# Sliding-window attention into a leaky-ReLU layer: the row sums of the softmax taken from pre-added overlaps, early values loaded four heads at a time, and two banks for the first units of chunk 9

## Chip, cores and metric

The kernel runs on one core of a Trainium2 chip. The metric is the device time of one execution in microseconds. Several runs are made and their median is the time of the kernel; one further execution is recorded by the hardware profiler, and the views below come from that one.

## What is computed

The reference is banded attention followed by a two-layer block. `q`, `k` and `v` are 8 batches x 8 heads x 576 positions x 64.

```
scores = q k^T / 8, kept where 0 <= i - j < 32            (heads 0 to 3, "plain")
                    or 0 <= i - j < 128 and i - j = 0 mod 4 (heads 4 to 7, "dilated")
attn   = softmax over the kept keys
x      = attn v, heads side by side: 4608 x 512
out    = max(0.01 h, h) w_out,  h = x w_in      (512 -> 2048 -> 512)
```

Inputs and output are float32; the products run on float16 operands.

## The kernel before

**Attention in units.** Two heads that are worked together make a "visit" (`VISITS`, two dilated ones first, then two plain ones), and a visit has two units of 288 queries (`unit`, L685). The keys of a unit stand in blocks of 64 per head (128 rows for the two heads), and a block meets only the queries that can see it: `steps` (L702 to L720) lists five blocks, each with its stretch of queries, 96, 80, 64 or 32 columns wide. Since a query in the overlap of two blocks is needed by both, the five stretches have 384 columns for 288 queries in a dilated unit and 416 in a plain one. A unit then runs: scores on TensorE (L732), exp on ScalarE into `ee` (L739), the mask as a product with a table in `con` on VectorE (L743; batches 0 and 1 add the mask on TensorE instead, L728), the product with a matrix of ones that gives the row sums (`t_sum_`, L754) and the product with the values (`t_v`, L756). Both of these are made by `second` (L747): five matmuls, one a block, that add into one bank at the place of their queries. Then come log and exp of the sums on ScalarE (L761, L763) and a multiplication into `xt` on VectorE (L774). There are 64 units, 8 in each batch.

**The two layers.** The tokens go in 12 chunks of 384. `up` (L784) makes the first layer of a chunk in 16 blocks of four matmuls. Chunks 9 to 11 use a Winograd-Strassen form with seven products (`up_seven`, L1157), each unit of it on three banks that go round in `last_seven` (L1244). `down` (L820) makes the second layer of the first four tiles plainly; all others go in groups of four through another seven-product form (`group`, L872; L922).

**Loads.** Batches 0 and 1 (`EARLY`) are loaded in an order written out by hand, `FIRST` (L29): `w0` to `w7` are pieces of `w_in`, `w8` to `w15` of `w_out`, `q` and `v` with batch and half are queries with keys and values (half 1 is the dilated heads), `r` is the last 64 positions, `c` is the mask table, and each "." is a further DMA of a `v` load named before. For a dilated half `load_v` (L510 to L516) makes six DMAs, and four casts of 64 x 576 (L521) put the values in their places. All of these are issued on SyncE's queue, in order; a DMA whose buffer is still in use holds back all behind it.

**What orders the work.** Nothing is executed as the Python calls come. Every operation is a task with engines that may take it, a cost, a delay and its dependencies (`add`, L76), and `_Plan.run` (L228) lists them: a forward pass places each task at the time when its engine is free, with the lowest due time first, a backward pass makes new due times, and the best of nine passes gives each engine one fixed order. `MARGIN`, `CALM`, `WHEN` and `RAMP` scale these costs and due times. A task that two engines may take goes to the one that ends it first by the plan. On the chip an engine runs its list in order and waits at each entry for its inputs.

Of the kernel before, what the change touches and what calls it, by code (L numbers as in the profile page):

```python
# [26 lines left out]
def _margin(name, at):  # L27
    return MARGIN[name] if at > CALM else 1.0
FIRST = ('w0 q01 r0 v01 . q00 . . . . w1 v00 . w2 w3 w4 w5 w6 w7 q11 r1 q10 v11 w8 w9 . '  # L29
         'w10 v10 . . . w11 . w12 . w13 . c . w14 w15')  # L30


def _constants():

    ident = np.eye(128, dtype=np.float16)
    key = np.arange(128)[:, None] % 64
    rel = np.arange(96)[None, :] - key
    band = (rel >= 0) & (rel < WIN)
# [6 lines left out]
    plain1 = [band] * 3 + [band[:, :64], band[:, 32:]]  # L45
# [204 lines left out]
def kernel(  # L250
# [54 lines left out]
    vst = [sbuf(f"vst{i}", [128, 1152], FP32) for i in range(NVS)]  # L305
    slots = sbuf("slots", [128, NT * TS])
    turned = [sbuf(f"turned{i}", [128, 640]) for i in range(NX)]
    ee = [sbuf(f"ee{i}", [128, 512]) for i in range(NE)]
# [180 lines left out]
    def load_v(b, g, prio, at_step=None):  # L489
# [5 lines left out]
        def when(x):  # L495
            n[0] += 1
            return at_step[n[0] - 1] if at_step else prio + x
        for hh in range(2):
# [184 lines left out]
    bank_at = [0]  # L683

    def unit(b, vi, u, prio, banks):  # L685
# [14 lines left out]
        if dil:  # L700
            n, steps = 384, []
            for ab in range(2):  # L702
                for r in range(2):
                    w = (96, 80)[ab]
                    steps.append((4 * ab + 2 * u + r, [[1, w]], (2 * u + r) * 144 + 64 * ab,
                                  96 * r if ab == 0 else 192 + 80 * r, w,
                                  144 * r + 64 * ab, [[1, w]]))
            steps.append((8, [[144, 2], [1, 16]], 2 * u * 144 + 128, 352, 32, 128, [[144, 2], [1, 16]]))
            bias = [(0, 192, 0, [[0, 2], [1, 96]]), (192, 160, 0, [[0, 2], [1, 80]]),
                    (352, 32, 96 + 32 * u, [[1, 32]])]  # L710
        elif u == 0:
# [3 lines left out]
            bias = [(0, 384, 0, [[0, 4], [1, 96]]), (384, 32, 0, [[1, 32]])]  # L715
        else:
            n = 416
            steps = [(s, [[1, 96]], 64 * s, 96 * (s - 5), 96, 64 * s - 288, [[1, 96]]) for s in (5, 6, 7)]
            steps.append((8, [[1, 64]], 512, 288, 64, 224, [[1, 64]]))
            steps.append((4, [[1, 64]], 288, 352, 64, 0, [[1, 64]]))  # L720
            bias = [(0, 288, 0, [[0, 3], [1, 96]]), (288, 64, 0, [[1, 64]]), (352, 64, 32, [[1, 64]])]
# [32 lines left out]
        t_sum_ = add("PE", 0.188, 0.25, [t_m, t_e, t_id], second(p_bank, lambda s: block_ones),  # L754
                     prio, 0.4, "z")
# [116 lines left out]
    def group(four, acts, at_time, split):  # L872
# [33 lines left out]
        def add_up(dst, a, b, op, deps, who, t_late=0.0):  # L906
            t = add("DVE", 0.63 if n_g > 3 else 0.78, 0.2, deps,
                    lambda e: ENG[e].tensor_tensor(out=dst, in0=a, in1=b, op=op),  # L908
                    at_time - 8 + t_late, 0.0, "A")
            for i in who:  # L910
                used[i].append(t)
            return t
# [134 lines left out]
    for i, step in enumerate(steps):  # L1047
        if step[0] == "v":
            rows[step] = [clock[0] + 1 + i]
            waiting += [step] * {"v01": 5, "v11": 5, "v00": 1, "v10": 3}[step]  # L1050
# [44 lines left out]
    U_SEVEN = (9, 10, 11)  # L1095
    HF, HT = DFF // 2, 192
# [60 lines left out]
    def up_seven(c, j0, batches, ts, acc, banks, when):  # L1157
# [70 lines left out]
        p7 = product(w_sum_of(3), x_sum_of(3), "Z", True, [s_t[3], ts[3][2]], 3)  # L1228
# [15 lines left out]
    def last_seven():  # L1244
# [8 lines left out]
        for order, c in enumerate(U_SEVEN):  # L1253
            batches = [[c // 3 * 2], [c // 3 * 2, c // 3 * 2 + 1], [c // 3 * 2 + 1]][c % 3]
            ts = x_sums(c, batches, order)
            for n in range(4):
                banks = [ready.pop(0) for _ in range(3)]
                up_seven(c, 2 * n, batches, ts, all_acts[c], banks, begins[c] + 2.5 * n)
                ready += before + [banks[1]]
                before = [banks[0], banks[2]]  # L1260

    n_g = 0
    for m in range(B // 2):
# [4 lines left out]
        if 3 * m not in U_SEVEN:  # L1268
            ups(3 * m, 0, 384, [e])
        if m == 0:  # L1270
# [6 lines left out]
        else:  # L1277
            attend(o, WHEN[o], 6.5)
            if 3 * m + 1 not in U_SEVEN:
                ups(3 * m + 1, 0, 384, [e, o])  # L1280
        if 3 * m + 2 not in U_SEVEN:
# [10 lines left out]
        while n_g < len(groups) and all(all_acts[c][0] for c, _ in groups[n_g]):  # L1292
            four = groups[n_g]
            group(four, all_acts, begins[four[-1][0] + 1] + four[-1][1] * 2.0, n_g == len(groups) - 1)
            n_g += 1
# [56 lines left out]
```

## Time and profile before

| What | us |
| --- | --- |
| median of 3 runs | 304.04 (304.03 to 304.31) |
| the profiled execution | 303.41 |
| span of its records | 301.5 |
| TensorE busy in the span | 288.6 |
| VectorE, ScalarE busy | 218.7, 217.1 |
| GpSimd busy | 136.7 |

The span is from the first to the last record; 1.9 us of the profiled execution lie outside it. PE is TensorE's matmuls, PEld its weight loads, DVE VectorE, ACT ScalarE, POOL GpSimd and SP SyncE; a "q" after a name means the engine's queue of instructions. L754 and the like are lines of the kernel. In a timeline a row has start, length, engine, line, operation, tiles, shape, count, and in brackets the idle time before it with what ended it. The length of a matmul includes its way through the array, so what a row of matmuls costs is better read from the chain of work or from the start of the next row.

### The profile page before, as it was taken

How to read it: one execution, taken by the hardware profiler on the slowest of the kernel's cores; microseconds unless marked ns; L12 is line 12 of the kernel's file. 1: busy time of each engine (PE TensorE's matmuls, PEld its weight loads, DVE VectorE, ACT ScalarE, POOL GpSimd, SP SyncE). 2: the span in 40 equal slices, each digit the busy share in tenths (PEclk: the TensorE clock that was granted, in tenths of full speed). 3: DMA queues.
4: the chain of work that ended last, by engine and by line, in shares of the span. 5: the costliest groups of instructions: out<-in, count | busy, mean ns of one | idle time of the engine just before them, and what ended most of it. 6: DMA issues, size and time to landing. Idle time of an engine off the chain costs nothing.

```text
span 301.5 us, 7912 instructions
## 1 busy us (share of the span) xinstructions
PE 288.6 (96%) x3038; PEld 227.9 (76%) x3038; DVE 218.7 (73%) x386; ACT 217.1 (72%) x509; POOL 136.7 (45%) x194
## 2 busy tenths in 40 slices
PE   5889989899999999999999999999999999999995
PEld 2466666568766789777777777877788999999984
DVE  5586464898568979876747779799964878587832
ACT  1497886568897775799688877688777778868321
POOL 5365434386678948778567984487000000000000
PEclk9999999999999999999999999999999999999999
DMA  7999999979988978997998999771201110011123
GB/s 241 303 339 371 293 275 282 158 152 177 161 176 164 235 160 164 207 163 157 193 167 200 161 219 170 142 183 36 72 2 49 57 37 1 10 65 70 37 104 105
DMA packets 156102, 47.17 MB, mean 156 GB/s; under 512 B 136864, under 2 KB 153376, under 8 KB 156064
## 3 DMA queue, kind: packets, MB, share of 16 engines
q1 hardware_dynamic: 155376, 46.04, 65.8%
q10 hardware_dynamic: 688, 0.63, 0.6%
q8 instruction: 23, 0.38, 0.5%
q14 instruction: 15, 0.12, 0.1%
HBM read 37.22 MB, written 9.44 MB: 155 GB/s over the span
## 4 chain that ended last, share of the span: by engine, by line
PE 81%; DMA 12%; DVE 2%; ACT 2%; SPq 1%; POOL 1%; issue 1%; DVEq 0%; POOLq 0%; ACTq 0%
PE hps L793 26%; PE fps L922 23%; PE tp L922 8%; DMA xt<-in_moe_w_out_dram 5%; DMA stg<-in_q_dram 5%; PE ops L750 4%; PE hps L1185 4%; PE ops L1185 4%; PE fps L832 3%; PE sps L750 2%; DMA vst<-in_v_dram 2%; PE ops L732 2%; PE sps L1185 1%; PE ops L922 1%; PE sps L732 1%; ACT slots L384 1%
## 5 line engine op out<-in xcount | busy, mean ns | idle before, releaser
L793 PE MATMUL hps<-xt,w_in 128*128 128x384 f16 (+1 forms) x616 | 107.4, 309 | 1.2 <-ACT gt L808 0.8
L808 ACT ACTIVATE gt<-hps 128x384 f16<-128x384 f32 (+1 forms) x154 | 69.1, 458 | 21.6 <-PE hps L793 19.8
L922 PEld LDWEIGHTS <-gt 128*128 128x128 f16 x768 | 72.4, 98 | 9.8 <-DVE gt L908 0.3
L793 PEld LDWEIGHTS <-w_in 128*128 128x128 f16 x640 | 56.4, 98 | 26.2 <-issue 1.9
L373 POOL CAST nat<-stg 128x576 f16<-128x576 f32 (+1 forms) x55 | 41.7, 779 | 30.2 <-DMA stg<-in_k_dram 20.7
L373 POOL CAST slots<-vst 64x576 f16<-64x576 f32 x53 | 47.0, 900 | 10.3 <-PE hps L793 4.4
L922 PE MATMUL fps<-w_out,gt 128*128 128x256 f16 x368 | 47.0, 272 | 0.0
L743 DVE TENSOR_TENSOR ee<-ee,con 128x384 f16<-128x384 f16 (+1 forms) x48 | 27.9, 582 | 13.4 <-ACT ee L739 13.1
L763 ACT ACTIVATE rc<-rc 128x288 f32<-128x288 f32 x64 | 27.7, 445 | 1.0
L774 DVE TENSOR_TENSOR xt<-ops,rc 128x288 f16<-128x288 f32 x42 | 18.8, 449 | 11.5 <-ACT rc L763 10.8
L386 POOL COPY slots<-turned 64x64 f16<-64x64 f16 (+2 forms) x41 | 21.6, 531 | 6.3 <-DVE turned L585 1.9
L739 ACT ACTIVATE ee<-ops 128x384 f16<-128x384 f32 (+1 forms) x41 | 20.5, 502 | 5.5 <-PE ops L732 5.5
L750 PEld LDWEIGHTS <-con 128*128 128x128 f16 x320 | 19.1, 98 | 4.8 <-issue 1.0
L732 PEld LDWEIGHTS <-slots 128*128 128x128 f16 x320 | 19.1, 97 | 4.5 <-ACT slots L384 0.2
L951 ACT COPY stg<-fps 128x512 f32<-128x512 f32 (+1 forms) x24 | 12.8, 533 | 11.4 <-PE fps L922 10.2
L750 PEld LDWEIGHTS <-slots 128*128 128x128 f16 x320 | 17.5, 97 | 3.5 <-issue 1.2
L761 ACT ACTIVATE rc<-ops 128x288 f32<-128x288 f32 x41 | 16.7, 411 | 4.1 <-PE ops L750 4.1
L585 DVE STREAM_TRANSPOSE turned<-nat 128x576 f16<-128x576 f16 x24 | 17.9, 760 | 1.3 <-POOL nat L373 1.3
L1212 ACT ACTIVATE gt<-slots 128x384 f16<-128x384 f32 x36 | 17.7, 526 | 1.4 <-DVE slots L1205 1.4
L832 PE MATMUL fps<-w_out,gt 128*128 128x512 f16 x64 | 16.6, 378 | 1.1 <-POOL w_out L373 0.7
L384 ACT COPY slots<-turned 64x576 f16<-64x576 f16 (+1 forms) x24 | 16.0, 666 | 1.1 <-DVE turned L585 0.8
L1185 PEld LDWEIGHTS <-stg 128*128 128x128 f16 x192 | 16.4, 98 | 0.4
(121 smaller groups left out, 504.1 us busy)
## 6 DMA issues: line engine op xcount, KB each, us to landing
out_dram<-osb SPq DMA_DIRECT2D x32, 256.0 KB, 2.6
stg<-in_q_dram SPq DMA_DIRECT2D x48, 144.0 KB, 3.6
stg<-in_k_dram SPq DMA_DIRECT2D x48, 144.0 KB, 3.4
vst<-in_v_dram SPq DMA_DIRECT2D x32, 128.0 KB, 3.1
vst<-in_v_dram SPq DMA_DIRECT2D x14, 288.0 KB, 4.3
gt<-in_moe_w_in_dram SPq DMA_DIRECT2D x6, 512.0 KB, 6.5
stg<-in_q_dram SPq DMA_DIRECT2D x3, 512.0 KB, 7.0
stg<-in_k_dram SPq DMA_DIRECT2D x3, 512.0 KB, 6.5
```

Source lines behind the costliest of these rows:

```text
L373: ENG[e].tensor_copy(out=dst, in_=src)
L386: ENG[e].tensor_copy(out=dst, in_=src)
L732: nc.tensor.matmul(p_bank[:, c:c + w], slot(tn, KB + 128 * s, 0, 128, [1, 128]), slot(tn, qx, 0, 128, *qd), start=first or not by_pe, stop ...
L739: lambda e: nc.scalar.activation(out=et[:, 0:n], in_=p_bank[:, 0:n], func=AF.Exp, scale=SCALE), prio)
L743: lambda e: nc.vector.tensor_tensor(out=et[:, 0:n], in0=et[:, 0:n], in1=con[:, table:table + n], op=ALU.mult), prio,
L750: nc.tensor.matmul(at(dst, 0, 128, o, *od), lhs(s), et[:, c:c + w], start=i == 0, stop=i == len(steps) - 1, skip_group_check=True)
L763: lambda e: nc.scalar.activation(out=rt, in_=rt, func=AF.Exp, scale=-1.0), prio)
L793: nc.tensor.matmul(ht[:, 0:n], at(w_in, 0, 128, vi * DFF + j // 2 * 256 + j % 2, [2, 128]), at(xt[m % 2], 0, 128, vi * 1152 + x0 + x, [1, n]),
L808: lambda e: nc.scalar.activation(out=gt[c % NG][:, j * n_c + x:j * n_c + x + n], in_=ht[:, 0:n], func=AF.Prelu, alpha=0.01),
L832: nc.tensor.matmul(ft, g[:, j * n_c + tt * 128:j * n_c + tt * 128 + 128], w_out[:, j * DM:j * DM + DM], start=(j == 0), stop=(j == NJ - 1))
L922: nc.tensor.matmul(bk[:, x:x + HN], tl[:, off + j * step:off + j * step + 128], rhs(j), start=first and x == 0 and j == 0, stop=j == HJ - ...
L1185: nc.tensor.matmul(b[:, i * HT:i * HT + HT], lhs(v, j0 + i), rhs(v), start=first and i == 0 and v == 0, stop=i == 1 and v == 1, skip_group ...
```

## The change

The query stretches of a unit are added up ahead of the product with ones: one or two additions (`both`) put the sum of two overlapping stretches behind the others in `ee`, at column 448 (`PLUS`), on VectorE or GpSimd. Then each query is streamed once (`sums_of`): 288 columns, in four matmuls (dilated), three (first plain unit) or two (second plain unit). This holds from batch 2 on (`PLUS_FROM`). So that the second plain unit's overlaps lie at one step, its fifth block comes first, in the mask table too.

The values of a dilated half of batches 0 and 1 are loaded in two DMAs in place of six, four heads at once, over 128 rows for the main part; ten casts then move them, eight of 64 x 256 and two of 64 x 128, in place of four. `FIRST` is another order: the first queries ahead of `w0`, the `v` pieces closer to their first one, `c` at the end.

The first two units of chunk 9 use two banks, the second one for both `Y` and `Z`, so that `p7` also waits for the addition that empties `Y`. `down_groups` is called after each `ups` and inside `last_seven`, not once in each turn of the loop. The scales of the plan have other values, and `RAMP` gives the early loads a delay that grows with their place.

```diff
-RAMP = 0
-WHEN = (0.0, 0.0, 40.0, 70.0, 100.0, 125.0, 150.0, 180.0)
+RAMP = 0.83
+WHEN = (0.0, 0.0, 40.0, 70.0, 100.0, 127.2, 150.0, 180.0)
-MARGIN = {'ACT': 1.045, 'DVE': 1.154, 'POOL': 1.018, 'PE': 1.0, 'SP': 1.0, 'DMA': 1.133, 'LAND': 1.15}
-CALM = 49.7
+MARGIN = {'ACT': 1.045, 'DVE': 1.13, 'POOL': 1.041, 'PE': 1.0, 'SP': 1.0, 'DMA': 1.139, 'LAND': 1.15}
+CALM = 38.0
-FIRST = ('w0 q01 r0 v01 . q00 . . . . w1 v00 . w2 w3 w4 w5 w6 w7 q11 r1 q10 v11 w8 w9 . '
-         'w10 v10 . . . w11 . w12 . w13 . c . w14 w15')
+FIRST = ('q01 w0 r0 v01 . q00 w1 v00 . w2 w3 w4 w5 w6 w7 q11 r1 v11 q10 w8 w9 . w10 v10 '
+         'w11 w12 . w13 . . w14 w15 c')
...
+        if g == 1 and b < EARLY:
+            t_main = load("SP", at(vs, 0, 128, 0, [256, 4], [1, 256]),
+                          dram(v, base, [4 * D, 128], [HS, 4], [1, 256]), 512, 1024, v_old, when(0.0))
+            t_last = load("SP", at(vs, 0, 64, 1024, [D, 4], [1, D]),
+                          dram(v, base + 512 * D, [D, 64], [HS, 4], [1, D]), 256, 256, v_old, when(0.01))
...
+            last = [cast(slot(t0, VB + hh + 1024, 64 * hh, 64 * hh + 64, [TS, 2], [2, D]),
+                         at(vs, 0, 64, 1024 + 128 * hh, [D, 2], [1, D]), 128,
+                         [t_last] + old[0] + old[1], prio, ("POOL", "DVE", "ACT"), 1.3) for hh in range(2)]
...
+                made = [cast(slot(t0 + j, VB + hh + 512 * i, 64 * hh, 64 * hh + 64, [128, 4], [2, D]),
+                             at(vs, 64 * i, 64 * i + 64, (2 * hh + j) * 256, [D, 4], [1, D]), 256,
+                             [t_main] + old[j], prio, ("POOL", "DVE", "ACT"), 1.3)
+                        for i in range(2) for hh in range(2)]
...
+            both = [(64, [[96, 2], [1, 32]], 192, [[80, 2], [1, 32]], 0, 32),
+                    (256, [[80, 2], [1, 16]], 352, [[16, 2], [1, 16]], 64, 16)]
+            sums_of = [(0, [[96, 2], [1, 64]], 0, [[144, 2], [1, 64]]),
+                       (PLUS, [[32, 2], [1, 32]], 64, [[144, 2], [1, 32]]),
+                       (224, [[80, 2], [1, 32]], 96, [[144, 2], [1, 32]]),
+                       (PLUS + 64, [[16, 2], [1, 16]], 128, [[144, 2], [1, 16]])]
...
-        t_sum_ = add("PE", 0.188, 0.25, [t_m, t_e, t_id], second(p_bank, lambda s: block_ones),
-                     prio, 0.4, "z")
+        if b < PLUS_FROM:
+            t_sum_ = add("PE", 0.188, 0.25, [t_m, t_e, t_id], second(p_bank, lambda s: block_ones),
+                         prio, 0.4, "z")
+        else:
+            t_both = []
+            for x, dx, y, dy, z, w in both:
...
+                    ENG[e].tensor_tensor(out=at(et, 0, 128, PLUS + z, *dz), in0=at(et, 0, 128, x, *dx),
+                                         in1=at(et, 0, 128, y, *dy), op=ALU.add)
+                t_both.append(add((("DVE", 0.08 + n_w * 0.001), ("POOL", 0.1 + n_w * 0.0011)), None, 0.2,
+                                  [t_m, t_e], fn, prio, 0.0, "m"))
...
+            t_sum_ = add("PE", 0.13, 0.25, [t_m, t_e, t_id] + t_both, add_over, prio, 0.4, "z")
...
-        p7 = product(w_sum_of(3), x_sum_of(3), "Z", True, [s_t[3], ts[3][2]], 3)
+        p7 = product(w_sum_of(3), x_sum_of(3), "Z", True,
+                     [s_t[3], ts[3][2]] + [h11[1]] * (banks[1] is banks[2]), 3)
...
-                banks = [ready.pop(0) for _ in range(3)]
+                if c == 9 and n < TWO:
+                    banks = [hps[n % 2], hps[1 - n % 2], hps[1 - n % 2]]
+                else:
+                    banks = [ready.pop(0) for _ in range(3)]
```

More of the change, by code (lines that the diff above doesn't have):

```diff
@@ L304 @@
     nat = [sbuf(f"nat{i}", [128, 1152]) for i in range(NNAT)]
-    vst = [sbuf(f"vst{i}", [128, 1152], FP32) for i in range(NVS)]
+    vst = [sbuf(f"vst{i}", [128, 1280], FP32) for i in range(NVS)]
     slots = sbuf("slots", [128, NT * TS])
     turned = [sbuf(f"turned{i}", [128, 640]) for i in range(NX)]
-    ee = [sbuf(f"ee{i}", [128, 512]) for i in range(NE)]
+    ee = [sbuf(f"ee{i}", [128, 640]) for i in range(NE)]
     rc = [sbuf(f"rc{i}", [128, 320], FP32) for i in range(NR)]
@@ L683 @@
     bank_at = [0]
+    PLUS, PLUS_FROM = 448, 2
     def unit(b, vi, u, prio, banks):
@@ L906, in add_up @@
         def add_up(dst, a, b, op, deps, who, t_late=0.0):
-            t = add("DVE", 0.63 if n_g > 3 else 0.78, 0.2, deps,
+            t = add("DVE", 0.63 if n_g[0] > 3 else 0.78, 0.2, deps,
                     lambda e: ENG[e].tensor_tensor(out=dst, in0=a, in1=b, op=op),
@@ L1095 @@
     U_SEVEN = (9, 10, 11)
+    TWO = 2
     HF, HT = DFF // 2, 192
@@ L1256, in last_seven, with down_groups @@
             for n in range(4):
-                banks = [ready.pop(0) for _ in range(3)]
-                up_seven(c, 2 * n, batches, ts, all_acts[c], banks, begins[c] + 2.5 * n)
-                ready += before + [banks[1]]
-                before = [banks[0], banks[2]]
-    n_g = 0
+                if c == 9 and n < TWO:
+                    banks = [hps[n % 2], hps[1 - n % 2], hps[1 - n % 2]]
+                else:
+                    banks = [ready.pop(0) for _ in range(3)]
+                    ready += before + [banks[1]]
+                    before = [banks[0], banks[2]]
+                up_seven(c, 2 * n, batches, ts, all_acts[c], banks, begins[c] + 2.5 * n)
+            down_groups()
+    n_g = [0]
+    def down_groups():
+        while n_g[0] < len(groups) and all(all_acts[c][0] for c, _ in groups[n_g[0]]):
+            four = groups[n_g[0]]
+            group(four, all_acts, begins[four[-1][0] + 1] + four[-1][1] * 2.0, n_g[0] == len(groups) - 1)
+            n_g[0] += 1
     for m in range(B // 2):
@@ L1269 @@
             ups(3 * m, 0, 384, [e])
+            if m:
+                down_groups()
         if m == 0:
@@ L1280 @@
                 ups(3 * m + 1, 0, 384, [e, o])
+                down_groups()
         if 3 * m + 2 not in U_SEVEN:
@@ L1291 @@
             part_free[0] = part_free[1] = rings["STG"][-1]
[L1292 to L1295, printed above, removed]
+        down_groups()
     order = plan.run()
```

33 lines of the change are left out of this document (27 added, 6 removed).

## The prediction, made before the result was known

> **What bounds the kernel now.** I read the page first, then busy time by stretches, then the waits of TensorE alone, then the chain of work.
>
> ```profile
> PE 288.6 (96%) x3038; PEld 227.9 (76%) x3038; DVE 218.7 (73%) x386; ACT 217.1 (72%) x509; POOL 136.7 (45%) x194
> ```
> ```profile
> 10.00:20.00 10.00, 7.71 (x107) 5.58 (x108) 6.40 (x15) 6.92 (x18) 5.81 (x8) 1.00 1.13 323
> 20.00:40.00 20.00, 19.25 (x217) 13.87 (x216) 11.99 (x29) 16.59 (x44) 8.96 (x15) 1.00 1.01 332
> 40.00:60.00 20.00, 17.27 (x189) 11.48 (x186) 13.11 (x23) 13.25 (x36) 7.73 (x10) 1.00 1.03 235
> 60.00:200.00 140.00, 139.94 (x1466) 107.43 (x1465) 109.75 (x177) 110.41 (x256) 100.16 (x138) 1.00 0.90 178
> 200.00:296.00 96.00, 96.00 (x1035) 85.52 (x1033) 70.31 (x131) 67.27 (x155) 8.90 (x11) 1.00 0.14 48
> ```
>
> The columns after the stretch are its length, then busy time of PE, PEld, DVE, ACT and POOL with counts, the granted clock, the DMA share and GB/s. From 60 to 296 us TensorE is never idle (139.94 of 140, 96.00 of 96) at full clock: what its list loses there the kernel gains, and a wait put into it is paid in full. Before 60 us it idles: 2.29 us from 10 to 20, 0.75 from 20 to 40, 2.73 from 40 to 60, with the DMA share over 1. So there are two stages, a head set by loads and a body set by TensorE.
>
> ```profile
> PE hps L793 <- ACT gt L808: 0.8, 2, 0.6
> PE fps L832 <- POOL w_out L373: 0.7, 1, 0.7
> ```
> ```profile
> 46.77 8.89 DMA xt<-in_moe_w_out_dram
> 55.66 0.05 issue
> 55.72 0.88 POOL w_out L373
> 56.60 0.04 issue
> 56.64 0.59 PE fps L832 x2
> ```
>
> The last wait that the head hands to TensorE is for `w_out`: its last piece lands at 55.66, POOL casts it, L832 starts at 56.64, and the body begins.
>
> **Part 1: the product with ones.** Here is the chain inside the body, and the count of units that mask on VectorE, which are the units from batch 2 on.
>
> ```profile
> 120.07 0.19 PE sps L750 x5
> 120.25 0.20 PE ops L750 x5
> 120.45 0.88 PE fps L922 x8
> 121.33 0.18 PE ops L750 x5
> 121.52 0.87 PE tp L922 x8
> 122.39 0.18 PE sps L750 x5
> 122.58 0.87 PE fps L922 x8
> 123.45 0.17 PE ops L732 x5
> 123.62 1.31 PE hps L793 x8
> ```
> ```profile
> L743 DVE TENSOR_TENSOR ee<-ee,con 128x384 f16<-128x384 f16 (+1 forms) x48 | 27.9, 582 | 13.4 <-ACT ee L739 13.1
> ```
>
> Eight matmuls of 384 columns take 1.31 us, so a column takes 0.426 ns. A dilated unit drops from 384 to 288 columns (0.041 us), a plain one from 416 to 288 (0.055 us). With 24 units of each, of the 48 that mask on VectorE, that is 0.98 + 1.31 = 2.29 us. A product of five takes 0.19 us on the mean of the four L750 rows, against 0.164 to 0.177 for its columns, so a matmul also has a few ns of its own, and 84 of 240 fall away (four, three or two in place of five). But the new ones are narrower, and no row shows a stretch of 32 or 64 alone. If a narrow one takes as long as one of 96 columns (0.041 us), a dilated product saves 0.01, a first plain 0.05, a second plain 0.065, together 1.6 us. If the time is all columns (0.123 a product), it is 48 x 0.065 = 3.1 us. I take **-2.4**, nearest the column count. It is on the path, since all 48 lie after 60 us.
>
> **Part 2: the head.** The mask table `c` moves behind the last two pieces of `w_out`, and the early dilated values are two DMAs, not six.
>
> ```profile
> 33.41 3.34 SPq L358 DMA_DIRECT2D vst<-in_v_dram  x4
> 44.54 0.63 SPq L358 DMA_DIRECT2D con<-consts  x1
> 45.92 0.74 SPq L358 DMA_DIRECT2D wst<-in_moe_w_out_dram  x1
> 46.77 0.36 SPq L358 DMA_DIRECT2D xt<-in_moe_w_out_dram  x1
> ```
> ```profile
> con<-consts SPq DMA_DIRECT2D x1, 400.0 KB, 7.2
> ```
>
> 400 KB at the 235 to 332 GB/s of the stretches are 1.2 to 1.7 us by which the last piece of `w_out` lands earlier. The mask is first wanted at 68.06 (L743 below), over 10 us after its new place, so the move costs nothing. Four loads of values held SyncE 3.34 us; four issues go in each of the two batches. Bytes and packet sizes stay, and the DMA engines are full, so I give this only 0.5 us. The ten casts in place of four carry the same elements; POOL has 11 and 12 us free in the two stretches from 20 to 60, which covers a fraction of a us of added starts. Putting the first queries ahead of `w0` may start attention earlier; I count nothing, as the last pieces of `w_in` come after the same bytes. Together **-2.0**. The bounds are a loss of 1.0, should a cast of values be late, and -5.8, all idle time of TensorE from 10 to 60.
>
> **Part 3: the first addition on GpSimd.** 72 additions are new. In the built order of the changed kernel 17 stand on VectorE and 55 on GpSimd, and ahead of GpSimd's first one stands one more instruction of line 797 that has no tile; I take it to make the engine ready for a kind of operation that it has not done before. GpSimd does no operation of two inputs in the trace of before, so neither is shown there. The place, in the trace of before:
>
> ```profile
> 66.29 0.23 POOL L386 COPY slots<-turned 64x64 f16<-64x64 f16 x1
> ...
> 69.70 0.85 POOL L373 CAST slots<-vst 64x576 f16<-64x576 f32 x1
> 72.72 1.27 POOL L373 CAST nat<-stg 128x576 f16<-128x576 f32 x2 [2.17 <-DMA stg<-in_k_dram]
> ```
> ```profile
> 68.06 1.79 DVE L743 TENSOR_TENSOR ee<-ee,con 128x384 f16<-128x384 f16 x2
> ```
> ```profile
> 68.00 0.34 PE L732 MATMUL ops<-slots 128*128 128x96 f16 x5
> 68.19 1.02 PE L832 MATMUL fps<-w_out,gt 128*128 128x512 f16 x4
> 69.05 0.82 PE L793 MATMUL hps<-xt,w_in 128*128 128x192 f16 x8
> 69.71 0.34 PE L750 MATMUL ops<-ee,con 128*128 128x96 f16 x5
> ```
>
> The extra instruction stands right behind the cast that ends at 70.55, then the two additions for the second unit of batch 2, then casts. On TensorE's new list the product that needs them comes behind these rows' work plus eight matmuls of 192 (0.66), eight of 256 (0.87), four of 192 (0.33) and the first unit's two products (0.34): 69.71 + 2.20 = 71.9. Everything behind that product on TensorE waits with it, and behind the additions GpSimd's casts of the next queries and keys. With part 2, GpSimd gets there 1.5 us earlier (69.05) and TensorE 2.0 (69.9). An addition of 64 or 32 columns takes between a copy of 64 x 64 (0.23) and two of them; 0.3 each, 0.6 for the pair. The load of the extra instruction is bounded by zero and by the longest fetch above, 8.89 us (a piece of `w_out` with the DMA engines full). The nearest row is the one in which an engine fetches what it needs for its functions:
>
> ```profile
> 0.73 1.28 ACT L1319 ACT_TABLE_LOAD   x1 [0.73 <-PEq L1336]
> ```
>
> With 1.28 the pair is done at 69.05 + 1.28 + 0.6 = 70.9, and TensorE waits **+1.0**. Each us more is a us more.
>
> The Trainium skill, GPSIMD Engine Reference, section 2.1 (Instruction dispatch), speaks against the change here: the first call of a freshly loaded kernel on this engine pays a load of about 6 us (5.95 measured) that no record of the profile shows. By that figure the time would be 4.7 us higher, 305.8, an estimate; no row of the trace of before can confirm or deny it.
>
> **The other 70 additions.** GpSimd's 55 at 0.3 are 16.5 us on top of 100.16 of 140, VectorE's 17 some 4 us on 109.75: both fit. A late one stops TensorE, as its list is fixed; I take **+0.5**, between 0 and 48 x 0.2 = 9.6, nearer the low end because both engines keep over 20 us free.
>
> **Chunk 9, `down_groups`, the plan's scales: 0.** TensorE's idle time there is nothing already (96.00 of 96), so no bank can be a gain. The new wait of `p7` is for one addition on VectorE behind the second product; if it is not covered by group matmuls ahead of it, two units pay some 0.5 us each (bounds -0.2 and +1.0).
>
> **Sum.** -2.4 - 2.0 + 1.0 + 0.5 = -2.9 us. The profiled execution was 303.41 (span 301.5 and 1.9 around it), so a like one comes to 300.5. The median, 304.04, stands 0.63 above it, which gives **301.1**.
>
> **Rivals.**
> *B, a long load on GpSimd (slower).* One mechanism at one place: the instruction ahead of the first addition holds GpSimd for several us at 69 us, and TensorE stands at the product of that unit. For a load of R us the wait is 69.05 + R + 0.6 - 69.9 = R - 0.25; the rest sums to -3.9. From R = 4.2 it eats all gains; at 4.5 to 8.9 the time is 304.4 to 308.8, at the middle 306.5. For it: the DMA share is 0.90 in this stage, fetches there take 3 to 9 us, and the additions stand on the path without cover (GpSimd's hole of 2.17 us behind its last cast is the only one). Against: the one fetch of tables in the trace takes 1.28 us.
> *C, the head gives nothing (nearly the same).* `w_out` may be held by the buffers and not by `c`. Then TensorE is at 71.9, GpSimd's pair at 70.55 + 1.28 + 0.6 = 72.4, and -2.4 + 0.5 + 0.5 = -1.4 gives 302.6; with a us or two of waits from the other order, 304.5. Against: the queue is full up to 55.66.
> *D, additions late everywhere (slower).* If each of the 48 sums waits 0.1 to 0.2 us, 4.8 to 9.6 replace the 0.5: 305.4 to 310.2. Against: both engines have room.
>
> **Chances.** Forecast 0.41 (298.5 to 303.2), B 0.36, C 0.15, D 0.08. A measurement of this kernel can tell about 0.2%, 0.6 us, from no change. Faster: 0.41, 0.02 of B, 0.09 of C, 0.52 together. Within: 0.04 of B and 0.03 of C, 0.07. Slower: 0.30 of B, 0.03 of C, 0.08 of D, 0.41. Cases of both signs hold much, so the range spans them: 298.5 (a load that is hidden, with 4 us from the head, would be below) to 308.0, which leaves out some of B's and D's upper ends, about 0.15 in all.
>
> **What would show it.** The products on line 804 should take 0.12 to 0.14 us in the chain. The last cast of `w_out` should end near 54.5. Around 70 us, the wait of TensorE for GpSimd's line 797 tells the forecast (about 1 us) from B (over 4), and GpSimd's gap ahead of its first addition is the load. From 80 to 296 TensorE should idle under 1 us; more, spread over line 804, is D. If TensorE's idle time from 40 to 60 is still 2.7, it is C. The forecast is wrong if the load is long, or if narrow matmuls cost as much as wide ones.

## The result, and the profile after

| | us |
| --- | --- |
| kernel before, median of 20 runs | 304.03 |
| changed kernel, median of 20 runs | 306.06 |
| ratio, 95% interval | 1.0074 (1.0048 to 1.010) |
| profiled execution of the changed kernel (span) | 306.33 (304.4) |

The change makes the kernel slower by 0.74%, where 1% faster was forecast. The ratios, here and below, leave out executions that a disturbance lengthened and the medians don't, so differences are taken from the ratios, at 303.9 us for the kernel before. These are the page's first line and the same five stretches as in the prediction, now of the changed kernel (columns as there):

```profile
PE 285.4 (94%) x2955; PEld 225.3 (74%) x2955; DVE 226.4 (74%) x411; ACT 217.4 (71%) x511; POOL 157.5 (52%) x251
```
```profile
10.00:20.00 10.00, 7.37 (x111) 5.32 (x111) 7.39 (x18) 7.20 (x22) 5.67 (x11) 1.00 0.92 264
20.00:40.00 20.00, 16.54 (x172) 11.07 (x170) 10.42 (x26) 14.50 (x34) 11.06 (x20) 1.00 1.05 350
40.00:60.00 20.00, 17.93 (x221) 13.53 (x220) 12.71 (x25) 15.46 (x44) 7.21 (x12) 1.00 1.02 241
60.00:200.00 140.00, 136.69 (x1377) 103.30 (x1376) 114.28 (x190) 108.69 (x252) 110.55 (x173) 1.00 0.88 174
200.00:296.00 96.00, 95.37 (x1010) 84.56 (x1009) 73.86 (x138) 67.25 (x155) 18.97 (x27) 1.00 0.16 51
```

TensorE has 3 us less to do (285.4, before 288.6), but from 60 to 296 us it now idles 3.31 + 0.63 = 3.94 us, where it idled 0.06. In the head it idles more from 20 to 40 us (3.46, before 0.75) and less from 40 to 60 (2.07, before 2.73). So the saved columns are there, and new waits have eaten them. Some of the waits of TensorE in the changed kernel:

```profile
PE tp L640 <- DVE slots L386: 1.9, 2, 1.5
PE tp L640 <- DVE nat L373: 1.8, 2, 1.4
PE fps L973 <- DVE gt L959: 1.3, 1, 1.3
PE sps L783 <- ACT ee L772: 1.2, 1, 1.2
PE ops L804 <- POOL ee L797: 1.2, 2, 0.6
PE ops L783 <- DVE ee L776: 0.5, 1, 0.5
```

L640 turns queries and keys (the head), L973 is a group product, L783 the product with the values, L804 the narrow product, L797 an addition. Only 1.5 us stand at the additions by name, 0.3 of it in a row that is not shown. The largest single place behind the head is here, on VectorE:

```profile
92.39 0.76 DVE L959 TENSOR_TENSOR rest<-gt 128x1024 f16<-128x1024 f16 x1
93.08 1.14 DVE L959 TENSOR_TENSOR pair<-gt 128x1024 f16<-128x1024 f16 x1
94.14 1.72 DVE L776 TENSOR_TENSOR ee<-ee,con 128x384 f16<-128x384 f16 x2
95.78 3.74 DVE L959 TENSOR_TENSOR gt<-gt,gt 128x1024 f16<-128x1024 f16 x2
99.43 1.25 DVE L959 TENSOR_TENSOR gt<-rest,gt 128x1024 f16<-128x1024 f16 x1
```

VectorE does not rest between these rows; two masks stand behind two group additions, and three more group additions behind the masks. TensorE waits first for the masks (0.52 us), then for the group additions (0.34 and 1.28).

### The profile page after: what moved, and what is told of

Same layout as the page of the kernel before. It is cut to its first block, busy times and chain, and to the rows that moved or that the text cites. A ratio compares the mean times of both kernels' runs of the same rounds, so it can differ in the third digit from the quotient of the medians.

```text
span 304.4 us, 7814 instructions
## 1 busy us (share of the span) xinstructions
PE 285.4 (94%) x2955; PEld 225.3 (74%) x2955; DVE 226.4 (74%) x411; ACT 217.4 (71%) x511; POOL 157.5 (52%) x251
## 4 chain that ended last, share of the span: by engine, by line
PE 67%; DVE 9%; DMA 7%; ACT 6%; SPq 4%; POOL 3%; issue 3%; POOLq 0%; DVEq 0%; ACTq 0%
PE hps L844 20%; PE fps L973 18%; PE tp L973 6%; DMA stg<-in_q_dram 6%; PE hps L1237 5%; PE fps L883 5%; SPq L358 4%; PE ops L1237 3%; PE ops L783 2%; DVE slots L386 2%; ACT slots L384 2%; PE ops L765 2%; DVE gt L959 1%; DVE ee L776 1%; PE sps L1237 1%
## 5 line engine op out<-in xcount | busy, mean ns | idle before, releaser
L844 PE MATMUL hps<-xt,w_in 128*128 128x384 f16 (+1 forms) x616 | 108.6, 309 | 1.0 <-ACT gt L859 1.0
L973 PEld LDWEIGHTS <-gt 128*128 128x128 f16 x768 | 72.6, 98 | 13.3 <-DVE gt L959 3.1
L373 POOL CAST slots<-vst 64x576 f16<-64x576 f32 (+2 forms) x60 | 50.3, 851 | 4.8 <-DMA vst<-in_v_dram 2.3
L973 PE MATMUL fps<-w_out,gt 128*128 128x256 f16 x368 | 47.0, 272 | 0.0
L373 POOL CAST nat<-stg 128x576 f16<-128x576 f32 (+1 forms) x53 | 38.2, 742 | 8.9 <-DMA stg<-in_q_dram 5.8
L797 POOL TENSOR_TENSOR ee<-ee 128x64 f16<-128x64 f16 (+2 forms) x55 | 23.3, 434 | 36.6 <-DVE ee L776 28.0
L776 DVE TENSOR_TENSOR ee<-ee,con 128x384 f16<-128x384 f16 (+1 forms) x48 | 25.2, 530 | 9.7 <-ACT ee L772 9.6
L386 POOL COPY slots<-turned 64x64 f16<-64x64 f16 (+2 forms) x38 | 20.8, 554 | 8.4 <-DVE turned L605 3.1
L783 PEld LDWEIGHTS <-slots 128*128 128x128 f16 x320 | 18.2, 97 | 4.8 <-issue 1.5
L1002 ACT COPY stg<-fps 128x512 f32<-128x512 f32 (+1 forms) x23 | 12.1, 528 | 9.6 <-PE fps L973 9.5
L384 ACT COPY slots<-turned 64x576 f16<-64x576 f16 (+1 forms) x27 | 17.8, 662 | 1.0 <-DVE turned L605 0.7
L973 PE MATMUL fps<-wst,gt 128*128 128x256 f16 x128 | 16.4, 272 | 1.3 <-DVE gt L959 1.3
L959 DVE TENSOR_TENSOR gt<-gt 128x1024 f16<-128x1024 f16 x21 | 16.4, 787 | 1.2 <-PE fps L973 1.1
```

Source lines behind the costliest of these rows:

```text
L373: ENG[e].tensor_copy(out=dst, in_=src)
L384: nc.scalar.copy(out=dst, in_=src)
L386: ENG[e].tensor_copy(out=dst, in_=src)
L776: lambda e: nc.vector.tensor_tensor(out=et[:, 0:n], in0=et[:, 0:n], in1=con[:, table:table + n], op=ALU.mult), prio,
L783: nc.tensor.matmul(at(dst, 0, 128, o, *od), lhs(s), et[:, c:c + w], start=i == 0, stop=i == len(steps) - 1, skip_group_check=True)
L797: ENG[e].tensor_tensor(out=at(et, 0, 128, PLUS + z, *dz), in0=at(et, 0, 128, x, *dx), in1=at(et, 0, 128, y, *dy), op=ALU.add)
```

## Experiments

Theory A: the additions are late and fill VectorE and GpSimd, which makes the stalls. Rival P: the new order of work makes them, with or without additions. Medians stand beside the kernel before on the same chip; ratios are to it, with 95% intervals.

### 1. The changed kernel, lists held fixed, without the additions

The instruction of an addition, in `fn`, becomes `pass`; the first kernel also has the old product (`second(p_bank, lambda s: block_ones)`), the second keeps the narrow one, the third has the additions and the old product. The fourth is planned anew:

```diff
-    PLUS, PLUS_FROM = 448, 2
+    PLUS, PLUS_FROM = 448, 8
```

> The changed kernel with its lists held fixed, but the 72 additions are not issued and the product with ones is the old one of five matmuls. Theory A (the additions cost more than they save: VectorE and GpSimd end late and TensorE stands, about 5 us of it between 60 and 220 us, against 2.4 us of columns saved): the stalls go, the columns come back, 306.1 - 5 + 2.4 = 303.5 us, and TensorE idles under 1.5 us from 60 to 200 (3.3 in the changed kernel). Rival P (the new order itself, from other scales and other calls, makes the stalls): they stay, 306.1 + 2.4 = 308.5 us, idle still about 3 us.

> The changed kernel with its lists held fixed and the new, narrow product with ones, but the 72 additions are not issued: the product reads the later stretch of each overlap alone, so the row sums leave out the earlier half of each overlap. Theory A: only the gain is left, 306.1 - 5 = 301.1 us, idle of TensorE under 1.5 us from 60 to 200. Rival P: as the changed kernel, 305.5 to 306.5 us. Against the kernel with the old product and no additions it tells what the saved columns are worth: 2.4 us by the prediction, 1.6 to 3.1 by its bounds.

> The changed kernel with its lists held fixed; the additions are made, but the product with ones is the old one of five matmuls and does not read them. It parts theory A in two. If TensorE waits for the additions themselves (one more step between mask and product), the stalls go as in the kernel without additions: 303.5 us. If the additions take time from the other work of VectorE and GpSimd, which is then late for TensorE, the stalls stay: 307.5 to 308.5 us. Rival P also gives 308.5 here, and is told apart by the kernel without additions.

> The changed kernel planned anew without any addition (the start batch of the additions set past the last one), so new loads, new order of loads, chunk 9 and scales stay. Theory A: stalls of the body gone, columns back, only the head's loss of about 0.6 us is left: 304.0 + 0.6 = 304.6 us. Rival P: the scales or the other edits make the stalls, 306 us or more.

| kernel (before: 303.77) | us | ratio |
| --- | --- | --- |
| no additions, old product | 308.99 | 1.0178 (1.0131 to 1.0226) |
| no additions, narrow product | 306.23 | 1.0096 (1.0058 to 1.0135) |
| additions, old product | 306.73 | 1.0106 (1.0050 to 1.0162) |
| planned anew without additions | 310.20 | 1.0200 (1.0143 to 1.0257) |

Theory A falls in this form. Without its additions the changed kernel takes 306.23, with them 306.06. Its lists lose the time even where nothing is added up, as P said. TensorE's idle time from 60 to 200 us agrees: 3.50 and 3.54 us in the first two kernels, 3.31 in the changed kernel. In the one profile of the third it is 1.42, with the same lists, so a wait seen in one execution need not be in the next. The narrow product gains 2.5 us without additions (1.0178 to 1.0096); with them it is 1.0 (1.0106 to 1.0074), which is within the noise.

### 2. One edit at a time, planned anew

The first is the kernel before with `both`, `sums_of` and the additions alone. The others are the changed kernel with one part as before: the scales; `FIRST` and the six loads; `down_groups` only at the end of each turn.

> The kernel before with the additions and the narrow product with ones as the only edit, planned anew with the old scales, loads and places of the group calls. If the additions by themselves gain what the pair of fixed-list runs says (2.8 us from narrow products, little lost in waits), this gives 304.0 - 2.4 = 301.6 us, between 301 and 302.5. If any new list loses several us because the plan does not know the lengths on the chip (theory J: the old list is a good one and each edit deals a new one), it gives 304 to 308 us with TensorE idle 2 us or more between 60 and 220.

> The changed kernel with the scales of the kernel before (RAMP, WHEN, MARGIN, CALM). If the scales make the stalls of the body (theory S: less margin for VectorE, and a margin that starts at 38 us in place of 49.7), the time falls to 301.5 to 303 us and the stall of 92 to 101 us goes. If not, it stays at 305 us or more.

> The changed kernel with the loads of the kernel before: its order and six transfers for the values of a dilated half. If the head is what costs (theory H: no gain of 2 us but a loss of about half a us, by the lag of TensorE at 60 us), the time falls by 0.5 to 2 us, to 304 to 305.5 us, and TensorE's busy time from 20 to 60 us rises from 34.5 to 36 or more. If the body alone costs, it stays at 306.

> The changed kernel with the group calls of the kernel before: once at the end of each turn of the loop. Theory G: the early calls put the additions of a group on VectorE into the stage of batch 3 (four between 92 and 101 us, where VectorE is busy 9.6 of 10 us); with the calls back the stall of 92 to 101 us goes, 306.1 - 3 = 303 us. If not, 305 us or more with stalls at other places.

| kernel (before: 303.91) | us | ratio |
| --- | --- | --- |
| before, additions alone | 308.97 | 1.0183 (1.0131 to 1.0235) |
| changed, old scales | 304.88 | 1.0045 (1.0009 to 1.0080) |
| changed, old loads | 308.99 | 1.0182 (1.0123 to 1.0240) |
| changed, old group calls | 308.35 | 1.0170 (1.0110 to 1.0229) |

Neither H (head) nor G (group calls) gave the fall that it asked for: with its part put back the kernel is slower still. S (scales) is 0.9 us (1.0074 to 1.0045), within the noise and not the 3 to 4.5 it asked for. The additions alone missed the 301.6 of the prediction's terms and came out a us above the 304 to 308 of theory J (any new list loses several us). All of them deal a new list, so none prices an edit by itself.

But the additions are not free in a new list. In the kernel before with the additions alone, 4.0 us of TensorE's waits end at one:

```profile
PE sps L804 <- POOL ee L797: 2.2, 1, 2.2
PE ops L804 <- POOL ee L797: 1.8, 5, 0.6
```

With the old loads such waits are 2.5 us, with the old group calls 3.1, with the old scales 1.1; in the changed kernel 1.5.

### 3. The list of the kernel before, held fixed

The additions are issued inside the mask's own task, so the plan does not see them and the order of everything else stays. The first kernel has the narrow product without additions; the third moves one transfer; the fourth has both edits. All but the third also have the wider buffers of the changed kernel and its order of blocks in the second plain unit.

```diff
+        def masked(e):
+            nc.vector.tensor_tensor(out=et[:, 0:n], in0=et[:, 0:n], in1=con[:, table:table + n], op=ALU.mult)
+            for x, dx, y, dy, z, w in both:
+                nc.vector.tensor_tensor(out=at(et, 0, 128, PLUS + z, [w, dx[0][1]], [1, w]),
+                                        in0=at(et, 0, 128, x, *dx), in1=at(et, 0, 128, y, *dy), op=ALU.add)
...
     order = plan.run()
+    q_sp = sorted((t for t in order if t.eng == "SP"), key=lambda t: (t.start, t.n))
+    n_c = q_sp.index(t_con[0])
+    t_con[0].start = q_sp[n_c + 3].start + 0.001
+    order.sort(key=lambda t: (t.start, t.n))
```

> The kernel before with its lists held fixed, and from batch 2 on the narrow product with ones, without any addition: it reads the later stretch of each overlap alone, so the row sums leave out the earlier half of each overlap. This measures the first term of the prediction by itself, in a list whose TensorE never idles from 60 to 296 us: 304.0 - 2.4 = 301.6 us (between 300.9 and 302.4 by the bounds of the term). If a list planned for the wide product gives part of it back in waits (TensorE ahead of exp, log and masks), less: 302.5 to 304.

> The same with the additions, all 72 on VectorE and each right behind its mask, so the lists of the kernel before stay fixed and nothing goes to GpSimd. Theory J (the new lists lose the time, not the additions): 301.6 us plus under 1 us of waits, 301.5 to 302.6, faster than both kernels. Theory A in its last form (the additions themselves cannot be hidden): 48 times 0.1 us or more of TensorE's waits, 306 us and above.

> The kernel before with one edit, the transfer of the mask table moved behind the last two pieces of w_out, lists held fixed. It measures the main piece of the prediction's second term: the last cast of w_out ends 1.2 to 1.7 us earlier and the time falls by as much, 302.3 to 302.8 us. If w_out is held by something else (its buffers, the casts), nothing: 303.5 to 304.5 us.

> The additions behind their masks and the mask table moved, lists of the kernel before held fixed. If the two terms add up, 304.0 - 2.0 - 1.4 = 300.6 us, and it beats both kernels; if the table's place gives nothing, as the kernel with the additions alone.

| kernel (before: 304.05) | us | ratio |
| --- | --- | --- |
| narrow product, no additions | 301.25 | 0.9868 (0.9802 to 0.9934) |
| additions behind the masks, on VectorE | 307.97 | 1.0086 (1.0040 to 1.0131) |
| mask table behind `w_out` | 303.51 | 0.9988 (0.9957 to 1.0019) |
| additions and table | 307.56 | 1.0117 (1.0073 to 1.0161) |

The narrow product is worth 4.0 us (2.0 to 6.0; 2.8 by the medians). Its page shows where 2.8 of it come from: TensorE is busy for 285.8 us, before for 288.6.

```profile
PE 285.8 (96%) x2954; PEld 225.3 (75%) x2954; DVE 217.3 (73%) x386; ACT 216.5 (72%) x509; POOL 136.8 (46%) x194
```

Additions on VectorE take 1.0086 - 0.9868, or 6.6 us, back (4.2 to 9.1 by the two intervals), so theory J's 301.5 to 302.6 was missed too: the additions are not free in the old list. The table's move gives nothing that can be measured. Where part of the 6.6 goes is seen around 70 us in the kernel with all additions (L771 mask, L773 addition, L793 narrow product):

```profile
69.67 0.34 DVE L771 TENSOR_TENSOR ee<-ee,con 128x384 f16<-128x384 f16 x1
69.72 0.26 PE L793 MATMUL ops<-ee,con 128*128 128x64 f16 x3 [0.39 <-DVE ee L773]
70.05 0.73 DVE L773 TENSOR_TENSOR ee<-ee 128x64 f16<-128x64 f16 x2
70.07 0.22 PE L793 MATMUL ops<-ee,con 128*128 128x128 f16 x1
70.75 0.26 PE L793 MATMUL ops<-ee,con 128*128 128x64 f16 x3 [0.46 <-DVE ee L773]
```

TensorE starts the product, stops after its first matmul until VectorE has added, and this twice in a row. A product that stops stands in the rows with 0.22 + 0.26 us, one that does not with 0.29 (L804, further below). So the stops lengthen TensorE's busy time too: the two profiles are 4.1 us apart (spans of 302.9 and 298.8), 1.9 of it idle time and 2.2 a longer busy time of the same 2954 matmuls. By stages TensorE stands most from 60 to 80 us. First the kernel before, then the one with all additions (here and below the columns end with the granted clock, DMA share and GB/s):

```profile
60.00:80.00 20.00, 19.94 (x218) 15.06 (x217) 16.62 (x27) 15.42 (x42) 15.44 (x21) 1.00 0.91 173
80.00:100.00 20.00, 20.00 (x197) 14.08 (x195) 14.89 (x24) 16.17 (x39) 14.14 (x20) 1.00 0.83 164
100.00:120.00 20.00, 20.00 (x221) 16.69 (x219) 17.78 (x28) 13.75 (x31) 14.54 (x18) 1.00 0.89 185
120.00:200.00 80.00, 80.00 (x838) 61.60 (x837) 60.46 (x101) 65.07 (x147) 56.05 (x82) 1.00 0.92 181
200.00:220.00 20.00, 20.00 (x212) 15.38 (x210) 19.41 (x33) 15.93 (x36) 8.90 (x11) 1.00 0.19 62
```
```profile
60.00:80.00 20.00, 18.35 (x185) 13.39 (x184) 18.42 (x33) 13.89 (x38) 15.38 (x21) 1.00 0.92 176
80.00:100.00 20.00, 19.62 (x181) 13.43 (x178) 15.51 (x29) 16.49 (x40) 13.54 (x21) 1.00 0.88 178
100.00:120.00 20.00, 19.98 (x207) 16.24 (x207) 18.62 (x36) 13.56 (x30) 12.55 (x15) 1.00 0.81 166
120.00:200.00 80.00, 79.94 (x812) 61.27 (x810) 70.24 (x135) 64.85 (x147) 56.31 (x81) 1.00 0.90 177
200.00:220.00 20.00, 19.83 (x201) 15.13 (x198) 19.33 (x39) 15.43 (x37) 10.62 (x13) 1.00 0.25 74
```

From 60 to 80 us VectorE was 83% busy already and goes to 92%, and TensorE idles 1.65 us. From 100 to 120 us VectorE is as full (89%, then 93%) and TensorE loses 0.02, so a full VectorE alone does not make the wait. From 120 to 200 us VectorE goes from 60.46 to 70.24 of 80 and TensorE loses 0.06.

### 4. Additions only where VectorE has room

The same kernel, with `both` used for some batches alone (`b >= 4`; `4 <= b <= 6`), and one with all additions whose product does not read them.

> The kernel before, lists held fixed, additions fused behind the masks of batches 4 to 7 alone (32 of the 48 units). Theory V (an addition is only hidden where VectorE has room; it had 9.25 of 10 us busy from 60 to 70, 9.44 from 110 to 120, 10.00 from 200 to 210, and 12.4 to 16.4 of 20 from 120 to 200): two thirds of the 2.8 us, less about 0.5 us at 200 to 220, 304.0 - 1.9 + 0.5 = 302.6 us, with TensorE idle under 0.3 us from 120 to 200. Rival W (each addition on the path costs TensorE the same wherever it stands: 6.7 us for 48 units in the kernel with all of them): 304.0 + 2/3 of (6.7 - 2.8) = 306.6 us.

> The kernel before, lists held fixed, all 72 additions on VectorE behind their masks, but the product with ones is the old one of five matmuls and does not read them. If the cost is VectorE's time (what stands behind the additions on it comes late), the waits stay: 308.0 + 2.8 = 310.8 us, or somewhat less since a wider product gives VectorE time. If the cost is the longer way from mask to product (about 0.2 to 0.5 us more before TensorE may start), most of it stays too for the first product that waits for the last addition, but not for the others: 304 to 306 us.

> As the kernel with additions from batch 4 on, but batch 7 left as it was, whose units run while VectorE is busy all the time (200 to 220 us). Theory V: half of 2.8 us and no waits, 304.0 - 1.4 = 302.6 us, the same as or better than the one with batch 7; TensorE idle 0 from 120 to 220. Rival W: 304.0 + half of 3.9 = 306.0 us.

| kernel (before: 303.87) | us | ratio |
| --- | --- | --- |
| additions in batches 4 to 7 | 303.00 | 0.9963 (0.9928 to 0.9999) |
| all additions, old product | 306.59 | 1.0089 (1.0052 to 1.0127) |
| additions in batches 4 to 6 | 303.66 | 0.9996 (0.9959 to 1.0032) |

W (the same price at each unit) asked for 306.6 and 306.0 and falls. V (room on VectorE) asked for 302.6 twice; the first agrees within its interval, the second is a us higher, with an interval that just leaves 302.6 out, and whether batch 7 pays is open. The kernel with batches 4 to 7 is ahead of both kernels, of the one before by 0.37% with an interval that ends just under 1, so hardly clear of the noise. Its stage from 120 us on:

```profile
120.00:200.00 80.00, 79.93 (x812) 61.33 (x810) 69.52 (x133) 65.34 (x149) 58.12 (x80) 1.00 0.90 177
```

The additions that nobody reads cost 2.7 us (1.0089; 1.6 to 3.9), as VectorE's time: the one long wait of TensorE behind 60 us there, 1.0 us, is for a group addition. By subtraction the other 3.9 of the 6.6 are the longer way from mask to product, but with the intervals of three kernels in it (1.2 to 6.6), and the two parts may overlap, since the wide product also gives VectorE time.

### 5. A nudge of the scales

```diff
-MARGIN = {'ACT': 1.045, 'DVE': 1.154, ...}
+MARGIN = {'ACT': 1.045, 'DVE': 1.150, ...}
```

The second kernel is the one before with all scales of the changed one, the third the changed one with 1.135 for 1.13.

> The kernel before with one scale changed by a hair (VectorE's margin 1.150 for 1.154), all operations the same. Theory J (the list is the thing: any edit that makes the plan anew deals another list, and the one in the kernel before is better than its neighbours): several us slower, 306 to 309 us, with waits of TensorE between 60 and 220 us. Theory N (lists are much alike, and what each edit costs is its own work): 303.4 to 304.6 us.

> The kernel before with the scales of the changed kernel (RAMP, WHEN, MARGIN, CALM) and nothing else. Theory J: 306 to 310 us, as with any other deal. Theory N, with the scales fitted to the additions: 304 to 305 us, since the same scales taken out of the changed kernel moved it by 1.2 us.

> The changed kernel with VectorE's margin at 1.135 for 1.13. Theory J: its list too is one of many; 305 to 310 us, so that the difference of 2 us between the two kernels says little of the edits. Theory N: 305.5 to 306.6 us.

| kernel (before: 304.42) | us | ratio |
| --- | --- | --- |
| before, nudged | 308.28 | 1.0130 (1.0090 to 1.0170) |
| before, new scales | 306.69 | 1.0069 (1.0036 to 1.0103) |
| changed, nudged | 309.41 | 1.0144 (1.0091 to 1.0198) |

Four thousandths on one scale, with the same operations, cost 4.0 us; half a hundredth costs the changed kernel 2.1 (1.0074 to 1.0144). That is J. The waits of the first nudged kernel stand in the head and the body, at lines that no edit touched:

```profile
PE tp L620 <- DVE nat L373: 1.9, 4, 0.9
PE fps L620 <- ACT slots L384: 1.5, 2, 0.8
PE tp L620 <- ACT slots L384: 1.2, 1, 1.2
PE ops L750 <- DVE ee L743: 0.7, 1, 0.7
```

## Why the prediction was wrong

**What bounds the kernel: right.** With the list kept, fewer columns on TensorE are less time, one for one within the noise.

**Part 1, -2.4: right.** With the list held TensorE is busy for 2.8 us less, and the time falls by 4.0 (2.0 to 6.0), with an interval that holds the forecast. The chain of the changed kernel has the product at 0.12 to 0.14 us, as said.

**Part 2, -2.0: wrong, and nothing is left of it.**

```profile
53.31 0.84 POOL L373 CAST w_out<-xt 128x512 f16<-128x512 f32 x1 [0.80 <-DMA xt<-in_moe_w_out_dram]
```

The last cast of `w_out` does end 2.4 us earlier, at 54.15 (before, its row in the prediction's chain ends at 56.60), near the 54.5 that was asked for. But there was less to gain there than 2.0: of TensorE's waits in the kernel before only 0.7 us stand at that cast (L832 for `w_out`, in the prediction's own rows), and the prediction names no other wait that its new order ends. And in the changed kernel TensorE was no longer waiting there. SyncE's queue at the same place, first before, then changed:

```profile
13.38 4.56 SPq L358 DMA_DIRECT2D gt<-in_moe_w_in_dram  x4
17.98 1.25 SPq L358 DMA_DIRECT2D wst<-in_moe_w_in_dram  x2
19.36 1.33 SPq L358 DMA_DIRECT2D stg<-in_q_dram  x1
```
```profile
12.74 7.48 SPq L358 DMA_DIRECT2D gt<-in_moe_w_in_dram  x4
20.27 1.51 SPq L358 DMA_DIRECT2D wst<-in_moe_w_in_dram  x2
21.90 0.56 SPq L358 DMA_DIRECT2D stg<-in_q_dram  x1
```

Behind the long loads of values four pieces of `w_in` hold SyncE for 7.48 us, not 4.56, and the first queries of batch 1 go out 2.5 us later. These are far ends of a spread: in eight profiles with the new loads the pieces took 6.1 to 7.5 us and the queries went out at 20.1 to 21.9, in eight with the list of the kernel before 4.5 to 5.8 us and 19.4 to 21.4. TensorE then waits at the turns of queries and keys (L640, above), between 30 and 45 us. The scores of the second unit of batch 2 start at 68.00 before and here in the changed kernel:

```profile
68.56 0.34 PE L765 MATMUL ops<-slots 128*128 128x96 f16 x5
```

So +0.56 in place of -2.0, in one execution of each, and that too has a spread: with the changed lists held these scores start at 66.40, 69.40 and 69.45, with the old list held and the old loads at 67.37 to 68.25. TensorE's idle time in the first 60 us says the same: 10.4 to 11.9 us in the four profiles with the changed lists, 8.5 to 11.0 in six with the old list and loads, on the mean 1.7 us more. No gain shows, and a loss of a us or two is likelier. The piece that I priced at 1.2 to 1.7, the table's place, gave 0.4 with an interval that holds zero (0.9957 to 1.0019). In that kernel's profile the last `w_out` transfer was issued at 47.53, not earlier than the 46.77 of before, but this execution was its slowest (306.65), and the unchanged queue gave 46.60 to 47.57 in six profiles; what took the time is not shown. What I left out is the question of what comes late next when a queue is put in another order.

**Part 3, +1.0 for the first addition on GpSimd: the load's size was right enough, the wait did not come, rival B is false.**

```profile
68.67 1.72 POOL L373 CAST slots<-vst 64x576 f16<-64x576 f32 x2
70.44 0.29 PE L804 MATMUL ops<-ee,con 128*128 128x128 f16 x4
70.88 1.35 POOL L797 TENSOR_TENSOR ee<-ee 128x64 f16<-128x64 f16 x2 [0.49 <-DVE ee L776]
76.81 0.51 POOL L797 TENSOR_TENSOR ee<-ee 128x64 f16<-128x64 f16 x2 [0.29 <-DVE ee L776]
```

The extra instruction is in the trace, as two MODIFY_POOL_CONFIG at 70.3 us. The first pair of additions behind it takes 1.35 us, a later one 0.51. The gap of 0.49 ahead of the pair ends with VectorE's mask, and part of a load could hide in it, so the load is at most 0.84 + 0.49, or 1.33, and the prediction had 1.28; B needed 4.2 or more. TensorE's view of waits has nothing at this place, so the +1.0 itself was not paid: TensorE too was later than I had it. The 6 us of the Trainium skill (GPSIMD Engine Reference, section 2.1) do not show here.

**The other 70 additions, +0.5: the reason was wrong.**

```profile
L797 POOL TENSOR_TENSOR ee<-ee 128x64 f16<-128x64 f16 (+2 forms) x55 | 23.3, 434 | 36.6 <-DVE ee L776 28.0 <-PE ops L765 5.6 <-PE hps L844 1.4
```

An addition takes 0.43 us on GpSimd, not 0.3. That matters less than the words "both engines keep over 20 us free", which is a mean over 140 us: by stretches of 20 VectorE had 3.4, 5.1 and 2.2 us free up to 120, and 0.6 from 200 to 220. Held in the old list, on VectorE, the additions cost 6.6 us, inside the bounds of 0 to 9.6 but nowhere near the low end that I took. In the changed kernel's own list they cost nothing that can be measured (ratio 1.0096 without, 1.0074 with).

**The plan's scales, 0: this is the step that failed most.** I priced each edit as if the rest of the order stood still. With the narrow product and no additions the old list has a ratio of 0.9868 and the changed one 1.0096: 6.9 us (5.0 by the medians) for the list, with the new loads, chunk 9 and the group calls in it. Two kernels with no edit but scales, planned anew, lost 4.0 and 2.1 us. So the +2.2 us of the change are -2.8 of TensorE's work and, as what is left, +5.0 from a list that waits more. In the two profiles TensorE stands 19.0 us of 304.4, before 12.9 of 301.5; 3.9 of these 6.1 us lie behind 60 us, where the prediction had 1.5 (its +1.0 and +0.5). Rival D (late additions) had the right time for a reason that holds for 1.5 us of waits at L804 at most; B's range held the time too, for a reason that is false.

The eight kernels that were planned anew say one thing more. Five have the additions and the narrow product (ratios 1.0045 to 1.0183, mean 1.0145), three have neither (1.0069 to 1.0200, mean 1.0133). The columns that the five save do not show in these means, and the waits that end at an addition are 1.1 to 4.0 us in the five, 2.8 on the mean. In a newly dealt list the additions thus seem to take back about what the narrow product saves; one profile of each cannot show more.

What stays open is why the list of the kernel before waits so little. That those tried here are worse is shown; which of its placements does it is not, nor whether its scales had been picked as the best of many, which would make any other list look worse. No experiment held the old list and put in the new loads alone.

## What to carry to other kernels

Where a planner deals the order, price an edit with the order held first (put the new instructions inside an existing task), then nudge a scale without any edit to see what a new deal costs. Look for room on an engine in the stretches where the new work falls, not on the mean of a stage. Work put between a producer and the engine that sets the end can be paid as a wait even when it is short: here 1.65 us where its engine was 17% free (60 to 80 us), and 0.06 where it was a quarter free (120 to 200).

## What the runs showed of the hardware

**VectorE slows beside GpSimd.** The five group additions of the stretch at 92 us took 0.76 to 2.20 us each, with GpSimd busy beside them. With GpSimd done, the same operation:

```profile
286.79 0.69 DVE L959 TENSOR_TENSOR gt<-gt 128x1024 f16<-128x1024 f16 x1
287.40 0.69 DVE L959 TENSOR_TENSOR rest<-gt 128x1024 f16<-128x1024 f16 x1
```

Over the changed kernel, 27 of them with no GpSimd work beside them took 0.68 to 0.69 us; 37 that ran beside it took 0.65 to 2.20, 0.97 on the mean. The Trainium skill (SBUF — State Buffer, section "Who interferes with whom") says that a VectorE instruction with two inputs in SBUF contends with a GpSimd instruction that reads SBUF; these rows agree. The plan has one length for each, which may be one reason why a list on the chip differs from the plan; that was not tried.

**A wait of TensorE can be paid twice.** In the changed kernel without additions and with the old product TensorE waits from 92.72 to 94.90 us:

```profile
92.00:94.00 2.00, 0.72 (x4) 1.00 0.34 81
94.00:96.00 2.00, 1.10 (x8) 0.66 1.16 263
96.00:98.00 2.00, 2.00 (x12) 0.50 1.15 183
98.00:100.00 2.00, 2.00 (x24) 0.99 1.18 252
```

The columns are the length, TensorE's busy time, clock, DMA share and GB/s. From 94.62 to 98.03 the granted clock is 0.50. TensorE is busy for 3.13 us of that, which at half the clock costs some 1.6 more (an estimate). Not each wait does this: waits of 2.17 us (the kernel before with additions alone, at 211 us) and 2.92 us (the kernel before with new scales, at 30 us) left the clock at 1.00, while one of 1.63 us (the changed kernel nudged, at 207 us) was followed by 0.50. In the seven places of all profiles here, between 12 and 290 us, where the clock went to 0.50, TensorE had been busy for only 1.35 to 1.57 of the 3.41 us before; stretches as idle also passed without it. Of the changed kernel's 20 runs, 11 have a mean clock of 0.994 or less, with a median of 306.88; the other nine have 304.54. The lower clock need not be all of that: the same split of the 101 executions of the kernel before in the experiments gives 304.55 (17) and 303.82 (84). The page "TensorE: Matmul & The Clock Gate" of the Trainium skill (section "What's actually happening") gives one idle window of about 3.4 us before the clock falls; here a wait of 2.18 was enough.
